# The first tile in halves, the small memory product in the start, and Wq and Wk one tile further ahead

## The chip, the cores and the metric

The kernel runs on one core of a Trainium2 chip. The time is device microseconds of one execution. Nearly all of it is work of TensorE. In the profile PE is TensorE (PEld its weight loads), DVE is VectorE, ACT is ScalarE, POOL is GpSimd, and SP is SyncE, which issues transfers. TensorE writes its results into banks of a memory called PSUM.

Two clocks are used. Lines of the profile count from the start of the span. Tables made from the trace count from the first warm-up matmul, which starts 1.38 us into the span in the kernel before. Such times are marked **W**.

## The reference, cut to what matters

```python
xn = _layernorm(x)                     # x: 2048 x 1024
out = x + A_ref(xn, mem0, Wq, Wk, Wv, Wo) + B_ref(xn, w1, w2, w3, w4)

# B_ref (mixer and MLP), the part that runs first:
h  = gelu(layernorm(xn) @ w1)          # "stage 1": 1024 x 1024 weights, 16 tiles of 128 tokens
hs = shifted(h) @ w2                   # "w2 stage"
x1 = xn + hs
b  = x1 + gelu(layernorm(x1) @ w3) @ w4

# A_ref: attention over segments of 32 tokens with 8 memory rows
h = concat([mem, xs]);  q, k, v = h @ Wq, h @ Wk, h @ Wv   # "V", then "attention" in five blocks
```

Of the kernel before, what the change touches and what calls it, by code (L numbers as in the profile page):

```python
# [23 lines left out]
P = 128  # L24
# [53 lines left out]
def kernel(  # L78
# [53 lines left out]
    ident = const_tile("c_ident", np.eye(P, dtype=np.float32))  # L132
    load_consts(1)
    eye9 = const_tile("c_eye9", np.concatenate([np.eye(M, dtype=np.float32), np.ones((M, 1), np.float32)], 1))
# [17 lines left out]
    nc.gpsimd.memset(sums[:], 1.0)  # L152
# [38 lines left out]
    with tc.manual_schedule(engines={mybir.EngineType.PE, mybir.EngineType.SP, mybir.EngineType.Pool}), ExitStack() as actx:  # L191
# [6 lines left out]
        with ExitStack() as bctx:  # L198
# [13 lines left out]
            with ExitStack() as hctx:  # L212
                psum0 = hctx.enter_context(tc.tile_pool(name="psum0", bufs=2, space=PSUM))
# [6 lines left out]
                with ExitStack() as p0:  # L220
# [7 lines left out]
                    def load_x(n):  # L228
                        if n < NT:
                            xts[n] = ring.tile([P, D], BF16, tag="xt", bufs=10, name=f"xt{n}")  # L230
                            nc.sync.dma_start(xts[n][:], x_v[:, n, :])

                    load_x(0)
# [13 lines left out]
                    def norm_stats(n, part=None):  # L247
# [14 lines left out]
                        nc.gpsimd.tensor_tensor(rr[:], ab[:], neghalf[:], op=ALU.pow)  # L262
# [26 lines left out]
                    def transposes(xn2, xn2T, jj, half, halves=False):  # L289
                        ps = psum0.tile([P, 4, P], F32, tag="tr")  # L290
                        for k in range(4):
                            nc.tensor.matmul(ps[:, k, :], xn2[:, (half * 4 + k) * P:(half * 4 + k + 1) * P], ident[:], start=True, stop=True)
                        step = 2 if halves else 4
                        for i in range(0, 4, step):
                            nc.scalar.copy(xn2T[:, jj, half * 4 + i:half * 4 + i + step, :], ps[:, i:i + step])
# [50 lines left out]
                    tr(0, 1, True)  # L346
                    norm_stats(1)
                    nc.gpsimd.memset(hTB[:, :, 0:2], 0.0)
                    nc.gpsimd.memset(hTB[:, :, S + 2:S + 4], 0.0)
                    load_consts(5)  # L350
# [12 lines left out]
                    def ahead(n):  # L363
# [3 lines left out]
                        norm1(n - 2)  # L367
# [5 lines left out]
                    def prep(n):  # L373
                        norm2_of(n)
                        norm_stats(n + 1)
                        norm1(n - 2)
# [38 lines left out]
            with ExitStack() as p3:  # L415
# [11 lines left out]
                def seg_sums(n):  # L427
# [3 lines left out]
                    with nc.allow_low_precision(reason="sums are accumulated in fp32 and rounded once"):  # L431
                        nc.vector.tensor_reduce(xb[:, :, 4 * n:4 * n + 4], xr[:].rearrange("p k (s t) -> p k s t", t=SEG), axis=AX.X, op=ALU.add)

                m0 = ring.tile([M, D], BF16, tag="nsq", bufs=1)
                nc.gpsimd.dma_start(m0[:], A_mem0[0])
                for c in range(7):
                    nc.sync.dma_start(w4_sb[:, 4 * c:4 * (c + 1), :], w4_v[:, 4 * c:4 * (c + 1), :])

                def mem_start():
                    ps9 = psum3.tile([P, KT, M + 1], F32, tag="vr")  # L440
                    for k in range(KT):
                        nc.tensor.matmul(ps9[:, k, :], m0[:, k * P:(k + 1) * P], eye9[:], start=True, stop=True)
                    nc.vector.tensor_copy(MZ[:, :, 0:M], ps9[:, :, 0:M])
                    nc.vector.tensor_tensor(xb[:, :, 0:1], ps9[:, :, M:M + 1], xb[:, :, 0:1], op=ALU.add)
# [83 lines left out]
                for tb in range(4):  # L528
# [18 lines left out]
                    for j in range(4):  # L547
# [16 lines left out]
                        elif n == 3:  # L564
                            mem_start()
# [168 lines left out]
        def stage_loads(Bs, hg, ready=()):  # L734

            cs_ = slice(hg * 512, (hg + 1) * 512)
            ws = [(w, None) for w in ready]
            ws += [(wtile(), src) for src in (Wq_v, Wk_v)[len(ready):]]
            (wq, _), (wk, _) = ws
            for w, src in ws[len(ready):]:  # L740
                for k0 in (0, 4):
                    loads.append(lambda w=w, src=src, k0=k0: nc.sync.dma_start(w[:, k0:k0 + 4, :], src[:, k0:k0 + 4, cs_]))
            return wq, wk
# [21 lines left out]
        ahead = stage_loads([nextB[0]], 0, first_w)  # L765
        for gi_, group in enumerate(groups):
# [3 lines left out]
            for hg in range(8):  # L770
# [3 lines left out]
                wq, wk = ahead  # L774
# [4 lines left out]
                if hg < 7:  # L779
# [239 lines left out]
```

## The kernel before: the parts that the change and the argument touch

Loads of the start. SP (`nc.sync`) and ScalarE (`nc.scalar`) issue them; w1 comes in quarters.

```python
def load_x(n):
    if n < NT:
        xts[n] = ring.tile([P, D], BF16, tag="xt", bufs=10, name=f"xt{n}")
        nc.sync.dma_start(xts[n][:], x_v[:, n, :])
load_x(0)
for c, q in ((0, nc.scalar), (2, nc.scalar), (1, nc.sync), (3, nc.sync)):
    if q is nc.sync:
        load_x(1 + c // 2)
    q.dma_start(w1_sb[:, 2 * c:2 * c + 2, :], w1_v[:, 2 * c:2 * c + 2, :])
# ... x tiles 3 to 6, w2 in quarters, x tiles 7 to 9; 10 to 12 follow in norm1
```

For each x tile: statistics on DVE, a power on POOL, and two normalisations. `norm2` is the input of stage 1. It runs on DVE up to tile 7 and on ScalarE from tile 8 on. Tiles 0 to 5 are then transposed by TensorE; from tile 6 on (`NPE = 6`) a **transposing transfer** (a DMA that transposes) issued by SP does it. `norm1` is kept for the residual, and stored to DRAM for attention.

```python
def norm2(n, xn2T, jj):
    xn2 = ring.tile([P, D], BF16, tag="xn2")          # three buffers
    if n < 8:
        ...                                           # DVE
    else:
        nc.scalar.activation(xn2[:], xts[n][:], ACTF.Identity, bias=nm2[:], scale=rr[:, 1:2])
    if n >= NPE:
        nc.sync.dma_start_transpose(xn2T[:, jj], xn2[:])

def norm1(n):
    xn = xn_keep[n // 4][:, n % 4]
    nc.vector.tensor_scalar(xn, xts[n][:], mv[:, 0:1], rr[:, 0:1], op0=ALU.subtract, op1=ALU.mult)
    nc.gpsimd.dma_start(xn_v[:, n, :], xn)            # 256 KB store

def transposes(xn2, xn2T, jj, half, halves=False):
    ps = psum0.tile([P, 4, P], F32, tag="tr")         # two banks
    for k in range(4):
        nc.tensor.matmul(ps[:, k, :], xn2[:, (half * 4 + k) * P:(half * 4 + k + 1) * P], ident[:], start=True, stop=True)
    step = 2 if halves else 4
    for i in range(0, 4, step):
        nc.scalar.copy(xn2T[:, jj, half * 4 + i:half * 4 + i + step, :], ps[:, i:i + step])

# stage 1 from tile 4 on takes two tiles at once; tile 9 is needed when tiles 8 and 9 start
stage1(3, 1, tiles2[2], {...: ahead(6) ... ahead(7)}, 1)
for n in range(13, NT):
    load_x(n)
def prep(n):
    norm2_of(n)
    norm_stats(n + 1)
    norm1(n - 2)
for n0 in range(4, NT, 2):
    ...                                               # prep(n0 + 4), prep(n0 + 5) between
    stage1(n0, 2, tiles2[n0], between)
```

The product of the memory rows with a small matrix (eight tiny matmuls, called `mem_start`) stands in the w4 stage. In attention the loads of Wq and Wk are made one group of heads ahead, into four buffers, and are put into SP's queue between the transposing transfers of the probabilities.

## Time and profile before

| | kernel before |
|---|---|
| times of its first three runs | 1509.06, 1513.19, 1509.02 us |
| span of the profiled run | 1507.1 us |
| TensorE busy | 1497.1 us |
| first stage 1 matmul (W) | 10.63 us |
| first w2 matmul (W) | 65.75 us |
| first V matmul (W) | 531.42 us |
| first matmul of attention's projections (W) | 752.44 us |
| first output matmul (W) | 873.86 us |

A landmark (when the first matmul of a stage starts) says how much time lies behind TensorE at that point. The difference of two landmarks is the length of a stage, holes included. The lines of the page, of the table of waits and of the order in time are shown and read in the prediction below. There `L305` is stage 1 of the first tile, `L315` stage 1, `L442` the eight small matmuls, `L658` the projections of attention.

### The profile page before, as it was taken

The numbers are of one execution on the slowest core, as the hardware profiler recorded it, in microseconds if no ns is written. First come the engines' busy times: TensorE is split into PE (matmuls) and PEld (weight loads), VectorE is DVE, ScalarE is ACT, GpSimd is POOL, SyncE is SP. The second block draws the span as 40 slices with busy tenths as digits, with TensorE's granted clock in tenths as the row PEclk, the third lists the DMA queues.
The fourth block names the chain that finished last, engine by engine and source line by source line (L and its number), as shares of the span: only waits on it lengthen the run. The fifth ranks groups of instructions, "written<-read, shape, count | busy, mean of one in ns | idle before, by whom it ended". The sixth has DMA issues, their size and how long they took to land.

```text
span 1507.1 us, 24242 instructions
## 1 busy us (share of the span) xinstructions
PE 1497.1 (99%) x9757; PEld 803.3 (53%) x9828; DVE 546.9 (36%) x1146; ACT 502.0 (33%) x1140; POOL 176.6 (12%) x247
## 2 busy tenths in 40 slices
PE   9999999999999999999999999999999999999999
PEld 7844444445454444444456645664665455545555
DVE  8382230100010112211246624651564166516642
ACT  5533103013012011111156614650663166406630
POOL 5241020211211221100000000001000100010001
PEclk9999999999999999999999999999999999999999
DMA  9699752453445777622389956992997298918911
GB/s 307 156 272 321 218 174 89 137 203 111 155 155 144 188 236 252 218 98 84 126 219 262 238 128 174 255 239 72 240 251 203 72 230 217 223 63 207 209 49 51
DMA packets 305410, 272.93 MB, mean 181 GB/s; under 512 B 156054, under 2 KB 272312, under 8 KB 305296
## 3 DMA queue, kind: packets, MB, share of 16 engines
q1 hardware_dynamic: 282800, 189.38, 50.4%
q0 software_dynamic: 21808, 80.85, 15.4%
q8 instruction: 79, 1.29, 0.4%
q10 hardware_dynamic: 688, 1.11, 0.2%
q14 instruction: 35, 0.29, 0.1%
HBM read 190.08 MB, written 45.29 MB: 156 GB/s over the span
## 4 chain that ended last, share of the span: by engine, by line
PE 98%; DVE 1%; issue 0%; DMA 0%; ACT 0%; POOL 0%
PE ps L658 30%; PE ps L592 15%; PE pso L716 15%; PE ps L533 13%; PE ps L559 13%; PE ps L397 4%; PE ps L315 3%; PE psS L673 2%; PE psO L697 2%; PE ps L856 1%; PE ps L485 1%; PE gps L468 0%; PE ps L454 0%; DVE st L256 0%; DVE st L259 0%
## 5 line engine op out<-in xcount | busy, mean ns | idle before, releaser
L658 PE MATMUL ps<-hTb,wt 128*128 128x396 bf16 (+2 forms) x2528 | 484.9, 342 | 0.0
L658 PEld LDWEIGHTS <-wt 128*128 128x128 bf16 x2528 | 236.7, 98 | 175.7 <-DMA wt<-in_A_Wq_dram 0.4
L592 PE MATMUL ps<-wt,xT 128*128 128x512 bf16 x1004 | 220.1, 379 | 1.1
L716 PE MATMUL pso<-wo_sb,oX 128*128 128x512 bf16 (+1 forms) x972 | 208.3, 372 | 1.1
L533 PE MATMUL ps<-xn3T,w_sb 128*128 128x512 bf16 x896 | 196.2, 379 | 0.0
L559 PE MATMUL ps<-w_sb,h3T 128*128 128x512 bf16 x873 | 194.1, 379 | 1.2
L592 PEld LDWEIGHTS <-xT 128*128 128x128 bf16 x1024 | 100.2, 98 | 120.8
L534 ACT ACTIVATE h3T<-ps 128x512 bf16<-128x512 f32 x112 | 66.9, 597 | 291.1 <-PE ps L533 290.2
L716 PEld LDWEIGHTS <-oX 128*128 128x128 bf16 x992 | 96.3, 98 | 107.6
L660 ACT CAST KT<-ps 128x462 bf16<-128x462 f32 (+2 forms) x160 | 81.8, 511 | 202.8 <-PE ps L658 198.7
L559 PEld LDWEIGHTS <-h3T 128*128 128x128 bf16 x896 | 87.1, 98 | 103.6
L533 PEld LDWEIGHTS <-w_sb 128*128 128x128 bf16 x896 | 86.6, 98 | 102.0
L679 DVE TENSOR_REDUCE sums<-sm 99x4 f32<-99x396 f32 (+2 forms) x176 | 97.6, 555 | 114.9 <-ACT sm L677 114.9
L662 ACT ACTIVATE QT<-ps 128x462 bf16<-128x462 f32 (+2 forms) x160 | 83.9, 525 | 120.3 <-PE ps L658 106.2
L594 ACT CAST Vs<-ps 128x512 bf16<-128x512 f32 x64 | 37.5, 586 | 232.1 <-PE ps L592 223.5
L675 DVE TENSOR_TENSOR sm<-psS,c_mask_reg_sb 99x396 f32<-99x396 f32 x152 | 86.7, 571 | 72.0 <-PE psS L673 71.7
L598 DVE CAST Vs<-ps 128x512 bf16<-128x512 f32 x64 | 44.3, 692 | 171.6 <-PE ps L592 166.0
L677 ACT ACTIVATE sm<-sm 99x396 f32<-99x396 f32 (+2 forms) x176 | 92.8, 527 | 34.9 <-DVE sm L675 27.9
L685 DVE TENSOR_TENSOR Pn<-sm,rs 99x396 bf16<-99x396 f32 (+2 forms) x176 | 98.9, 562 | 6.4 <-DVE rs L681 0.5
L723 POOL DMA_DIRECT2D out_dram<-ot x30 | 16.4, 548 | 698.2 <-DVE ot L722 698.1
L560 DVE TENSOR_TENSOR R<-ps,R 128x512 f32<-128x512 f32 x32 | 22.0, 690 | 182.1 <-PE ps L559 172.5
L722 DVE TENSOR_TENSOR ot<-pso,Rt 128x512 bf16<-128x512 f32 (+1 forms) x33 | 22.2, 675 | 166.6 <-PE pso L716 162.3
(127 smaller groups left out, 1049.5 us busy)
## 6 DMA issues: line engine op xcount, KB each, us to landing
wt<-in_A_Wq_dram SPq DMA_DIRECT2D x76, 512.0 KB
wt<-in_A_Wk_dram SPq DMA_DIRECT2D x76, 512.0 KB
wt<-in_A_Wv_dram POOLq DMA_DIRECT2D x24, 1024.0 KB, 6.4
V_scratch<-Vs SPq DMA_DIRECT2D x32, 512.0 KB
V<-V_scratch SPq DMA_DIRECT2D x40, 384.0 KB
R_scratch<-x POOLq DMA_DIRECT2D x16, 512.0 KB, 4.1
R<-R_scratch SPq DMA_DIRECT2D x16, 512.0 KB
R_scratch<-R POOLq DMA_DIRECT2D x16, 512.0 KB, 3.5
```

The lines of the kernel that those rows point to most:

```text
L533: nc.tensor.matmul(ps[:].rearrange("p (n t) -> p n t", t=P), w3_sb[:, k, f * P:(f + 1) * P], xn3T[tb][:, :, k, :], start=(k == 0), stop=(k ...
L534: nc.scalar.activation(h3T[:, f, :], ps[:], ACTF.Gelu_apprx_tanh)
L559: nc.tensor.matmul(ps[:], h3T[:, f, j * P:(j + 1) * P], w4_sb[:, f, ch * 512:(ch + 1) * 512], start=(f == 0), stop=(f == FT - 1))
L592: nc.tensor.matmul(ps[:], xT[:, m4 * 4 + j, k, :], wv[:, k, :], start=(k == 0), stop=(k == KT - 1))
L658: nc.tensor.matmul(ps[:, :nb], w[:, k, hh * P:(hh + 1) * P], B["hT"][:, k, :nb], start=(k == 0), stop=(k == KT - 1))
L660: nc.scalar.copy(dst[:, hh, :], ps[:, :nb])
L662: nc.scalar.mul(dst[:, hh, :], ps[:, :nb], scale)
L675: nc.vector.tensor_tensor(sm[:T, :, :T], S3, t["mask"][:].unsqueeze(1).to_broadcast((T, 4, T)), op=ALU.add)
L677: nc.scalar.activation(e[:T, :, :T], sm[:T, :, :T], ACTF.Exp, scale=LN2)
L679: nc.vector.tensor_reduce(ss, e[:T, :, :T], axis=AX.X, op=ALU.add)
L685: nc.vector.tensor_tensor(Pn[:T, :, :T], e[:T, :, :T], rs[:T, :].unsqueeze(2).to_broadcast((T, 4, T)), op=ALU.mult)
L716: nc.tensor.matmul(self.ps[:, :self.w], self.oX[0][:, h, self.oX[1] + self.gl * P:self.oX[1] + (self.gl + 1) * P], wo_sb[:, h, self.cc], s ...
```

## The change

Its intent: get the first tile through sooner (two half loads on two queues, an identity made on the core and not loaded, a power split in two, four PSUM banks for the transposes), move the eight small matmuls from the w4 stage into a hole at the start, take one `norm1` out of tile 9's path, and load Wq and Wk of attention one tile further ahead, with a fifth buffer in three blocks. The load of x tile 12 also moves to POOL's queue.

```diff
-    ident = const_tile("c_ident", np.eye(P, dtype=np.float32))
+    ident = cpool.tile([P, P], BF16)
+    nc.vector.memset(ident[:], 1.0)          # ... then affine_select on POOL
-                psum0 = hctx.enter_context(tc.tile_pool(name="psum0", bufs=2, space=PSUM))
+                psum0 = hctx.enter_context(tc.tile_pool(name="psum0", bufs=4, space=PSUM))
-                            nc.sync.dma_start(xts[n][:], x_v[:, n, :])
+                            if n == 0:
+                                nc.scalar.dma_start(xts[n][:, 512:], x_v[:, n, 512:])
+                                nc.sync.dma_start(xts[n][:, :512], x_v[:, n, :512])
+                            else:
+                                (nc.gpsimd if n == 12 else nc.sync).dma_start(xts[n][:], x_v[:, n, :])
-                        nc.gpsimd.tensor_tensor(rr[:], ab[:], neghalf[:], op=ALU.pow)
+                        for c in (slice(1, 2), slice(0, 1)) if n == 0 else (slice(0, 2),):
+                            nc.gpsimd.tensor_tensor(rr[:, c], ab[:, c], neghalf[:, c], op=ALU.pow)
 # transposes: one bank for each copy, not one for two
                     tr(0, 1, True)
+                    ps9 = psum.tile([P, KT, M + 1], F32, tag="mm", bufs=4, name="ps9")
+                    for k in range(KT):
+                        nc.tensor.matmul(ps9[:, k, :], m0[:, k * P:(k + 1) * P], eye9[:], start=True, stop=True)
 ...                                           # mem_start in the w4 stage is deleted
                     def prep(n):
                         norm2_of(n)
                         norm_stats(n + 1)
+                        if n == 8:
+                            norm1(n - 3)      # ahead(7) no longer does it
                         norm1(n - 2)
 ...
-                if hg < 7:
-                    ahead = stage_loads(Bs, hg + 1, ...)
+                while len(ws) < min(now + (5 if now < 44 else 4), 16 * len(SEGS)):
+                    load_w()                  # every fifth tile into the free buffer "oXb"
```

More of the change, by code (lines that the diff above doesn't have):

```diff
@@ L130, in load_consts @@
             nc.gpsimd.dma_start(t[:], d.ap())
-    ident = const_tile("c_ident", np.eye(P, dtype=np.float32))
-    load_consts(1)
-    eye9 = const_tile("c_eye9", np.concatenate([np.eye(M, dtype=np.float32), np.ones((M, 1), np.float32)], 1))
+    ident = cpool.tile([P, P], BF16)
+    nc.vector.memset(ident[:], 1.0)
+    eye9 = cpool.tile([M, M + 1], BF16)
+    c0 = cpool.tile([P, KT, 1], F32)
     mask_first = const_tile("c_mask_first", _tile_mask(3, True))
@@ L151 @@
     sums = cpool.tile([P, NTILE * 8, 4], F32)
-    nc.gpsimd.memset(sums[:], 1.0)
     SH = (-1, -1, 1, 1, -2, -2, 2, 2)
@@ L230, in load_x @@
                             xts[n] = ring.tile([P, D], BF16, tag="xt", bufs=10, name=f"xt{n}")
-                            nc.sync.dma_start(xts[n][:], x_v[:, n, :])
+                            if n == 0:
[3 more added lines that the diff above has]
+                                (nc.gpsimd if n == 12 else nc.sync).dma_start(xts[n][:], x_v[:, n, :])
+                    m0 = hTB[:M, 0, 16:16 + D]
+                    nc.gpsimd.dma_start(m0, A_mem0[0])
+                    nc.gpsimd.affine_select(ident[:], ident[:], [[-1, P]], ALU.is_equal, 0.0, base=0, channel_multiplier=1)
+                    nc.gpsimd.memset(eye9[:, M:M + 1], 1.0)
+                    nc.gpsimd.tensor_copy(eye9[:, 0:M], ident[:M, :M])
                     load_x(0)
@@ L289, in transposes @@
                     def transposes(xn2, xn2T, jj, half, halves=False):
-                        ps = psum0.tile([P, 4, P], F32, tag="tr")
-                        for k in range(4):
-                            nc.tensor.matmul(ps[:, k, :], xn2[:, (half * 4 + k) * P:(half * 4 + k + 1) * P], ident[:], start=True, stop=True)
                         step = 2 if halves else 4
                         for i in range(0, 4, step):
-                            nc.scalar.copy(xn2T[:, jj, half * 4 + i:half * 4 + i + step, :], ps[:, i:i + step])
+                            ps = psum0.tile([P, 4, P], F32, tag="tr")
+                            for k in range(step):
+                                c = (half * 4 + i + k) * P
+                                nc.tensor.matmul(ps[:, k, :], xn2[:, c:c + P], ident[:], start=True, stop=True)
+                            nc.scalar.copy(xn2T[:, jj, half * 4 + i:half * 4 + i + step, :], ps[:, :step])
                     def stage1_k(xn2T):
@@ L346 @@
                     tr(0, 1, True)
+                    ps9 = psum.tile([P, KT, M + 1], F32, tag="mm", bufs=4, name="ps9")
+                    for k in range(KT):
+                        nc.tensor.matmul(ps9[:, k, :], m0[:, k * P:(k + 1) * P], eye9[:], start=True, stop=True)
                     norm_stats(1)
+                    nc.vector.tensor_copy(MZ[:, :, 0:M], ps9[:, :, 0:M])
+                    nc.vector.tensor_copy(c0[:], ps9[:, :, M:M + 1])
                     nc.gpsimd.memset(hTB[:, :, 0:2], 0.0)
                     nc.gpsimd.memset(hTB[:, :, S + 2:S + 4], 0.0)
-                    load_consts(5)
+                    load_consts(4)
+                    nc.gpsimd.memset(sums[:], 1.0)
                     for n in range(1, 6):
@@ L366, in ahead @@
                         norm_stats(n + 1, 1)
-                        norm1(n - 2)
+                        if n == 6:
+                            norm1(n - 2)
                     stage1(3, 1, tiles2[2], {0: [lambda: tr(4, 0)], 2: [lambda: tr(4, 1), lambda: ahead(6)], 4: [lambda: tr(5, 0)], 5: [lambda: tr(5, 1), lambda: ahead(7)]}, 1)
@@ L432, in seg_sums @@
                         nc.vector.tensor_reduce(xb[:, :, 4 * n:4 * n + 4], xr[:].rearrange("p k (s t) -> p k s t", t=SEG), axis=AX.X, op=ALU.add)
-                m0 = ring.tile([M, D], BF16, tag="nsq", bufs=1)
-                nc.gpsimd.dma_start(m0[:], A_mem0[0])
+                    if n == 0:
+                        nc.vector.tensor_tensor(xb[:, :, 0:1], c0[:], xb[:, :, 0:1], op=ALU.add)
                 for c in range(7):
                     nc.sync.dma_start(w4_sb[:, 4 * c:4 * (c + 1), :], w4_v[:, 4 * c:4 * (c + 1), :])
-                def mem_start():
-                    ps9 = psum3.tile([P, KT, M + 1], F32, tag="vr")
-                    for k in range(KT):
-                        nc.tensor.matmul(ps9[:, k, :], m0[:, k * P:(k + 1) * P], eye9[:], start=True, stop=True)
-                    nc.vector.tensor_copy(MZ[:, :, 0:M], ps9[:, :, 0:M])
-                    nc.vector.tensor_tensor(xb[:, :, 0:1], ps9[:, :, M:M + 1], xb[:, :, 0:1], op=ALU.add)
                 def unit_vb(hg):
@@ L563 @@
                                 spec_step(depth)
-                        elif n == 3:
-                            mem_start()
                         elif n > 3:
@@ L732, in load_some, with load_w @@
                 loads.pop(0)()
-        def stage_loads(Bs, hg, ready=()):
+        ws = first_w + second_w
+        def load_w():
+            n = len(ws)
+            src, hg = (Wq_v, Wk_v)[n % 2], n // 2 % 8
             cs_ = slice(hg * 512, (hg + 1) * 512)
-            ws = [(w, None) for w in ready]
-            ws += [(wtile(), src) for src in (Wq_v, Wk_v)[len(ready):]]
-            (wq, _), (wk, _) = ws
-            for w, src in ws[len(ready):]:
-                for k0 in (0, 4):
-                    loads.append(lambda w=w, src=src, k0=k0: nc.sync.dma_start(w[:, k0:k0 + 4, :], src[:, k0:k0 + 4, cs_]))
-            return wq, wk
+            ws.append(abig.tile([P, KT, 512], BF16, tag="oXb", name=f"w{n}") if n < 48 and n % 5 == 3 else wtile())
+            for k0 in (0, 4):
+                loads.append(lambda w=ws[-1], k0=k0: nc.sync.dma_start(w[:, k0:k0 + 4, :], src[:, k0:k0 + 4, cs_]))
         def tick(us, blocked=None):
@@ L764 @@
         nextB = {b: block_setup(b) for b in groups[0]}
-        ahead = stage_loads([nextB[0]], 0, first_w)
         for gi_, group in enumerate(groups):
@@ L773 @@
                     load_some(len(loads))
-                wq, wk = ahead
+                now = 16 * gi_ + 2 * hg
+                wq, wk = ws[now:now + 2]
                 QTs = [qkv.tile([P, 4, B["nb"]], BF16, tag="QT", name=f"QT{B['b']}") for B in Bs]
@@ L778 @@
                     nextB = {b: block_setup(b) for b in groups[gi_ + 1]}
-                if hg < 7:
-                    ahead = stage_loads(Bs, hg + 1, second_w if (gi_, hg) == (0, 0) else ())
-                if hg == 7 and gi_ + 1 < len(groups):
-                    ahead = stage_loads([nextB[b] for b in groups[gi_ + 1]], 0)
+                while len(ws) < min(now + (5 if now < 44 else 4), 16 * len(SEGS)):
+                    load_w()
                 Vs = [qkv.tile([P, len(B["tiles"]), 512], BF16, tag="V", bufs=3, name=f"V{B['b']}") for B in Bs]
```

## The prediction

> **What bounds the kernel now.** I read the page's busy shares first, then the table of who TensorE waited for, then the order in time of the places where it waited.
>
> ```profile
> PE 1497.1 (99%) x9757; PEld 803.3 (53%) x9828; DVE 546.9 (36%) x1146; ACT 502.0 (33%) x1140; POOL 176.6 (12%) x247
> PE warm L332 <- DVE wz L326: 1.4, 1, 1.4
> PE ps L292 <- DVE xn L271: 0.8, 1, 0.8
> PE ps L315 <- ACT hTB L317: 0.5, 1, 0.5
> PEld L442 <- issue: 0.4, 1, 0.4
> PEld L658 <- DMA wt<-in_A_Wq_dram: 0.4, 1, 0.4
> ```
>
> TensorE is busy for 1497.1 of 1507.1 us, and a busy TensorE need not be at its rate, so I checked the rate: I took the start-to-start distance of all consecutive matmuls in the trace and subtracted columns/2.4 GHz + 2.5 ns. Counting the places where a matmul record is plainly missing as no loss, what is left over in the whole run is: 0.96 us between the last warm-up matmul and the first transpose (5.96 to 7.14), 0.30 us between the transposes and the first real matmul (7.64 to 7.99), 0.6 us at 31.4 to 32.2, 0.34 us around the eight small matmuls of L442 at 219 us, and a spread of under 0.25 us per pair of lines elsewhere. After the last matmul there is the output's tail to 1507.1, which the change does not touch. So all that any change of order can win here is about 2.2 us, 0.15% of the time. The wait for Wq in the second wait table is on the weight load; no pair of matmul starts around 789 us, where it falls, is further apart than its columns explain (one pair has 167 ns, exactly one missing record). Weight loads run ahead, so that wait was hidden.
>
> The start, in order of time for TensorE:
>
> ```profile
> 1.38 4.96 PE L332 MATMUL warm<-wz 128*128 128x512 bf16 x12 [1.38 <-DVE wz L326]
> 7.14 0.72 PE L292 MATMUL ps<-c_ident_sb,xn 128*128 128x128 bf16 x8 [0.79 <-DVE xn L271]
> 7.99 2.84 PE L305 MATMUL ps<-xn2T,w_sb 128*128 128x128 bf16 x48
> 10.67 0.61 PE L292 MATMUL ps<-c_ident_sb,xn 128*128 128x128 bf16 x8
> 11.12 1.06 PE L305 MATMUL ps<-xn2T,w_sb 128*128 128x128 bf16 x16
> ...
> 4.03 0.69 DVE L256 BATCH_NORM_STATS2 st<-xt 128x6 f32<-128x512 bf16 x1 [2.71 <-DMA xt<-in_A_x_dram]
> ```
>
> The reader is to see that the path to the first transpose is x tile, statistics, power on POOL, normalisation; and that from 7.99 us on TensorE runs without a hole. The DMA side of the same stretch (last columns: granted clock, DMA share, GB/s):
>
> ```profile
> 2.00:3.00 1.00, 1.00 (x3) 0.30 (x2) 0.00 (x0) 1.00 (x1) 0.61 (x1) 1.00 0.78 178
> 3.00:4.00 1.00, 1.00 (x4) 0.39 (x3) 0.00 (x0) 0.25 (x2) 0.00 (x0) 1.00 0.99 377
> 8.00:10.00 2.00, 2.00 (x36) 2.00 (x36) 1.11 (x5) 0.77 (x3) 0.83 (x4) 1.00 1.05 389
> ```
>
> From 3 us on the DMA engines are full, at 377 to 389 GB/s. The trace's semaphore increments give the landings: x tile 0 at 4.01, the four quarters of w1 at 5.28, 8.79, 8.54 and 10.83 us (in the order in which TensorE needs them). It needs them at 7.99, 7.99+16x0.056=8.88, 9.78 and 11.12. The second and the last have 0.1 and 0.3 us to spare.
>
> **What the Trainium skill says.** "TensorE: Matmul & The Clock Gate", section "Wait — 56ns, not 53.3ns?", gives N/2.4 GHz plus about 2.5 ns start to start when warm. The trace agrees: fifty 512-column matmuls from 67.57 to 78.36 us are 215.8 ns each; my bound of 2.2 us rests on it. "DMA: Bandwidth & Descriptors", section "Issuing engines are not separate DMA queues", says transfers issued by scalar, sync and gpsimd run on the same 16 DMA engines and interleave, so a second issuer saves only issue time. The trace agrees: with two issuers active the sum stays at 377 to 389 GB/s. "Perfetto Trace Analysis", section "Matmuls", wants independent groups in different PSUM banks so that evacuation overlaps the next group. Here the first ScalarE copy starts at 7.57, after all four transposes of its bank, which is what two copies out of one bank look like. "GPSIMD Engine Reference", section "2.1 Instruction dispatch", puts about 6 us on the first call after a library is loaded. The trace bounds that lower: the pool configuration is at 2.53 us and the first power starts at 5.91, 0.08 us after its input, so at most 3.3 us.
>
> **The change part by part.**
>
> First tile. x tile 0 comes as two halves of 128 KB on two queues, ahead of w1. Today the first 128 KB of it have been started by 2.57 us and the second only by 3.49. I expect the first statistics at about 3.3 and the second at about 3.9 (today 4.63), an estimate from those packet times. The power on POOL is split; one of one column takes 0.57 us (L405) against 0.73 for two, 0.16 less. So the first transpose moves from 7.14 by 0.7+0.16 to about 6.3, just where the warm-up matmuls leave TensorE (last one started at 5.96). The eight L442 matmuls (8x0.035=0.28 us) are put after the transposes, where TensorE has its 0.30 us hole anyway, so the first real matmul still comes about 0.85 us after the first transpose: about 7.2 instead of 7.99. But the last quarter of w1 must be there for the last sixteen of those matmuls. All bytes ahead of it are the same 2.8 MB through the same full engines, so it lands near 10.8 again, and the L305 matmuls that start at 11.12 today can start at about 10.9. **Gain 0.2 to 0.25 us, not 0.8.** The identity is now made on POOL, not loaded, and has until about 6 us; the transfer of the identity landed at 6.6 us, so this had to go for the transposes to start earlier.
>
> L442 moved. At 219 us it cost 0.34 us. In its new place it is hidden. **Gain 0.34 us.** One DVE addition and two small copies from PSUM fall into DVE's 0.8 us waits for the power.
>
> The stall at 31.4 us. TensorE waits for a bank that ScalarE frees:
>
> ```profile
> 30.64 1.24 ACT L273 ACTIVATE xn<-xt,nm,rr 128x1024 bf16<-128x1024 bf16 x1 [2.05 <-DVE mv L260]
> 31.79 0.91 ACT L317 ACTIVATE hTB<-ps 128x256 bf16<-128x256 f32 x3
> 32.20 35.09 PE L315 MATMUL ps<-xn2T,w_sb 128*128 128x256 bf16 x320 [0.54 <-ACT hTB L317]
> ```
>
> ScalarE sat 2.05 us before the normalisation of tile 8 (L273), in order, with the eviction behind it. The releaser named is DVE, but the wait just before it in ScalarE's queue ended at 30.56, and 30.54 is when the transposing transfer of tile 6 landed, 5.57 us after its issue at 24.96. It was issued as soon as tile 6 was normalised. DVE's chain runs about 0.6 us earlier in the new kernel, TensorE only 0.2, so the transfer lands at about 29.95 and the eviction ends near 31.6 where TensorE asks at 31.46. Moving the normalisation of tile 5 behind tile 9's statistics takes 0.54 us of DVE off tile 9's path, not off tile 8's, so it adds nothing to this wait. **Gain about 0.4 of the 0.54 us.**
>
> Wq and Wk one tile ahead. Loads per stage are the same, each buffer is freed at the same place; the fifth buffer exists only because a tile lies idle in blocks 0 to 2. It removes the 0.4 us wait of the weight load, which cost TensorE nothing. **Gain 0 to 0.1 us.**
>
> Sum: 0.2+0.34+0.4+0.1=1.04, so 1509.06-1.1=**1508.0 us**.
>
> **The rivals.** (1) The transfers don't bind at the start: two queues fill the engines before 3 us, where they moved only 178 GB/s, and the last quarter of w1 lands 0.5 us earlier. Then the start gives up to 0.8 us and the stall is fully gone: 1507.1. Against it: the scalar queue's first packet came only at 2.95 us although issued at 0.76. (2) The start gives nothing: the library load stands ahead of the identity's making on POOL, and the power waits for it; or the quarter of w1 at 8.79 (0.1 us to spare) stalls TensorE, and the transpose transfer still takes its 5.6 us: only L442's 0.34 us remains, 1508.7. (3) The longer look-ahead of Wq and Wk matters in runs that the profile did not show: one of the three runs took 1513.19, and if that was a late weight tile, the new kernel loses this tail but not the median. (4) SBUF or queue order makes a new wait in attention; the lists of instructions show SP's loads only moved earlier, so I give it little.
>
> **Range and chances.** TensorE's floor puts the best case near 1506.8; nothing in the change adds TensorE work, so the worst is about the time of before plus the spread of runs, 0.3 us. Eight in ten: 1507.0 to 1509.2. A change of 2% would need 30 us, fifteen times the whole loss: same 0.985, and one run in a hundred for something unforeseen that slows.
>
> **What would show it.** First transpose near 6.3 and first L305 matmul near 7.2; a new short hole before the L305 matmuls of the last quarter of w1, released by its transfer; no small matmuls at 219 us; the wait for ScalarE at 31 us below 0.2 us; no Wq wait near 789 us and otherwise the same attention. The prediction is wrong if that hole is absent (rival 1), if the first transpose stays after 7 us (rival 2), or if attention changes by more than 0.2 us.

## The result, and the profile after

Six runs of each kernel, with the kernel before at 1509.69 us median (1509.02 to 1513.19) and the changed one at **1509.2 us median** (1508.82 to 1510.15). The ratio is 0.9994, with a 95% interval of 0.9981 to 1.0007. A ratio is the mean time of one kernel's fast runs over that of the other's of the same rounds, so it is not quite the ratio of the medians. With the later calls there are 11 runs of the changed kernel (mean 1509.48, median 1509.39) and 38 of the kernel before (mean 1509.84): 0.35 us less, with a standard error of 0.23 us from the spread of the runs. That is below the 1.1 us forecast, and not clearly different from nothing. About 0.15 us of it lies outside the profiled span: the time is 2.04 to 2.20 us longer than the span before, and 1.91 to 1.99 us after.

The page of the changed kernel shows the same TensorE work:

```profile
PE 1497.4 (99%) x9757; PEld 803.7 (53%) x9828; DVE 547.0 (36%) x1148; ACT 502.1 (33%) x1140; POOL 175.5 (12%) x250
```

Its table of waits, TensorE's rows (total us, times, longest), answers to the one of before:

```profile
PE warm L343 <- DVE wz L337: 1.5, 1, 1.5
PE ps L316 <- DMA w_sb<-in_B_w_dram: 1.0, 1, 1.0
PE ps L326 <- DMA xn2T<-xn: 0.9, 1, 0.9
PE psO L708 <- ACT KT L671: 0.5, 1, 0.5
```

Of the waits shown of before only the warm-up's is left, and three others have come: for a quarter of w1, for a transposing transfer, and one in attention. The profiled run took 1510.15 us and was the slowest of the six, so a second profile was needed before believing any of them. First the start of this one, in order of time, TensorE only:

```profile
6.57 0.79 PE L305 MATMUL ps<-ident,xn 128*128 128x128 bf16 x8
7.29 0.35 PE L360 MATMUL ps<-eye,hTB 8*128 8x9 bf16 x8
7.58 1.07 PE L316 MATMUL ps<-xn2T,w_sb 128*128 128x128 bf16 x16
9.64 1.96 PE L316 MATMUL ps<-xn2T,w_sb 128*128 128x128 bf16 x32 [0.99 <-DMA w_sb<-in_B_w_dram]
11.44 0.61 PE L305 MATMUL ps<-ident,xn 128*128 128x128 bf16 x8
11.88 1.06 PE L316 MATMUL ps<-xn2T,w_sb 128*128 128x128 bf16 x16
```

The transposes start at 6.57 (7.14 before), the eight small matmuls fit behind them, and the first real matmul comes at 7.58 (7.99 before). Then TensorE waits for the second quarter of w1. Its sixteen semaphore increments came spread from 7.22 to 9.59 us; in the kernel before they came from 8.28 to 8.79. The windows of the same stretch (last columns: granted clock, DMA share, GB/s):

```profile
2.00:3.00 1.00, 1.00 (x4) 0.33 (x3) 0.00 (x0) 0.72 (x1) 0.53 (x4) 1.00 0.74 245
3.00:4.00 1.00, 1.00 (x3) 0.30 (x2) 0.43 (x1) 0.76 (x2) 0.00 (x0) 1.00 1.04 273
8.00:10.00 2.00, 1.01 (x19) 0.83 (x17) 1.18 (x5) 0.23 (x1) 1.44 (x5) 1.00 1.05 405
```

The transfers move 245 GB/s at 2 to 3 us where they moved 178. At 8 to 10 us the transfers are full, as before, and TensorE is idle for half of it. The second new wait with a cause in view is in attention's first block (order in time, DVE and TensorE):

```profile
797.81 0.57 DVE L696 TENSOR_TENSOR Pn<-sm,rs 99x396 bf16<-99x396 f32 x1 [1.19 <-DMA PT<-Pn]
797.85 0.34 PE L708 MATMUL psO<-PT,V 99*128 99x99 bf16 x4 [0.55 <-ACT KT L671]
```

DVE waited 1.19 us for a transposing transfer of probabilities to free its buffer, and TensorE lost 0.71 us (start-to-start distance less the columns' time) just then.

### The profile page after: what moved, and what is told of

It is laid out like the page before. It is cut to its first block, busy times and chain, and to the rows that moved or that the text cites. A ratio compares the mean times of both kernels' runs of the same rounds, so it can differ in the third digit from the quotient of the medians.

```text
span 1508.2 us, 24250 instructions
## 1 busy us (share of the span) xinstructions
PE 1497.4 (99%) x9757; PEld 803.7 (53%) x9828; DVE 547.0 (36%) x1148; ACT 502.1 (33%) x1140; POOL 175.5 (12%) x250
## 4 chain that ended last, share of the span: by engine, by line
PE 98%; DMA 1%; issue 0%; SPq 0%; ACT 0%; DVE 0%
PE ps L669 30%; PE ps L603 15%; PE pso L727 15%; PE ps L546 13%; PE ps L572 13%; PE ps L417 4%; PE ps L326 3%; PE psO L708 2%; PE psS L684 2%; PE ps L865 1%; PE ps L498 1%; DMA w_sb<-in_B_w_dram 1%; PE ps L467 0%; PE gps L481 0%; DMA xn2T<-xn 0%
## 5 line engine op out<-in xcount | busy, mean ns | idle before, releaser
L669 PE MATMUL ps<-hTb,wt 128*128 128x462 bf16 (+2 forms) x2272 | 439.6, 344 | 0.0
L669 PEld LDWEIGHTS <-wt 128*128 128x128 bf16 x2272 | 212.7, 98 | 159.9
```

Source lines behind the costliest of these rows:

```text
L669: nc.tensor.matmul(ps[:, :nb], w[:, k, hh * P:(hh + 1) * P], B["hT"][:, k, :nb], start=(k == 0), stop=(k == KT - 1))
```

## The experiments

All kernels gave correct results. Each is run for five rounds (four in two cases), beside the kernel before. Two readings carry the argument: the landmarks, and **holes**, which are start-to-start distances of TensorE's matmuls less columns/2.4 GHz + 2.5 ns, with plainly missing records left out.

### 1. The changed kernel and the kernel before once more

No edit. This is for a second profile of each.

> The changed kernel itself again, for a second profile and five more times. Theory A (the hole at 8.4 us behind the second quarter of w1, and the 1.1 us stall at 39 us behind a transposing transfer, are luck of one execution, the slowest of three): here both are smaller, together under 1.0 us, the first w2 matmul comes less than 66.3 us after the first warm-up matmul (it was 66.83), and the median is under 1509.0. Theory B (both belong to the new order of transfers): both are there again at 0.7 us or more each, the first w2 matmul at 66.5 to 67, the median 1509 to 1509.5.

> The kernel before itself, for a second profile and the noise of one comparison. First w2 matmul 65.6 to 66.0 us after the first warm-up matmul (65.75 in its first profile) if its start is repeatable; over 66.3 if the start wanders from execution to execution by as much as the change moved it. Ratio to itself within 0.0007 of 1.

Changed kernel again: 1509.88 us median, above the ranges of both theories, ratio 1.0 (0.9987 to 1.0014). Kernel before again: 1509.98, ratio to itself 1.0006 (0.9992 to 1.002), and its first w2 matmul at W 66.03, 0.03 above the expected range. TensorE at the start of the changed kernel, second profile:

```profile
6.59 0.72 PE L305 MATMUL ps<-ident,xn 128*128 128x128 bf16 x8 [0.15 <-DVE xn L281]
7.24 0.35 PE L360 MATMUL ps<-eye,hTB 8*128 8x9 bf16 x8
7.53 2.89 PE L316 MATMUL ps<-xn2T,w_sb 128*128 128x128 bf16 x48
10.25 0.61 PE L305 MATMUL ps<-ident,xn 128*128 128x128 bf16 x8
10.83 1.07 PE L316 MATMUL ps<-xn2T,w_sb 128*128 128x128 bf16 x16
```

The wait for the second quarter is gone (it landed at W 6.93, for 8.12 in the first profile): so late a landing was of one execution. What stays is the short hole before 10.83, where the last sixteen matmuls wait for the last quarter of w1. It landed at W 9.30, and they start at W 9.35.

The stall in stage 1 did not go. Kernel before, second profile, ScalarE and TensorE:

```profile
30.92 1.24 ACT L273 ACTIVATE xn<-xt,nm,rr 128x1024 bf16<-128x1024 bf16 x1 [2.57 <-DMA xn2T<-xn]
32.48 9.77 PE L315 MATMUL ps<-xn2T,w_sb 128*128 128x256 bf16 x88 [1.06 <-ACT hTB L317]
```

Changed kernel, second profile, the same two engines:

```profile
29.95 1.24 ACT L283 ACTIVATE xn<-xt,nm,rr 128x1024 bf16<-128x1024 bf16 x1 [1.63 <-DVE ab L270]
39.90 2.34 PE L326 MATMUL ps<-xn2T,w_sb 128*128 128x256 bf16 x20 [1.24 <-DMA xn2T<-xn]
```

In before ScalarE's normalisation of tile 8 waits for tile 6's transposing transfer, ScalarE's eviction stands behind it, and TensorE loses 1.22 us at W 30. In the changed kernel ScalarE starts 1 us sooner and TensorE loses only 0.29 us there. But 7 us later it loses 1.41 us, now directly for a transposing transfer, that of tile 9. Theory A (luck) falls for stage 1 and holds for the start; the first w2 matmul, at W 66.36 for 66.83, lies between what the two expected.

### 2. Each half of the change alone

Look-ahead only: the last part of the diff on the kernel before. Start only: the rest of the diff.

```diff
 # look-ahead only: before, with
+                while len(ws) < min(now + (5 if now < 44 else 4), 16 * len(SEGS)):
+                    load_w()
 # start only: the changed kernel, with
-                while len(ws) < min(...): load_w()
+                if hg < 7:
+                    ahead = stage_loads(Bs, hg + 1, ...)
```

> The kernel before with only the Wq and Wk look-ahead of the change. If the look-ahead is worth nothing, as predicted (0 to 0.1 us): 1509.1 to 1509.7 and its profile has no stall of TensorE over 0.3 us in attention. If its earlier loads make the new 0.7 us stall at 797 us (a transposing transfer of attention slowed by weights): the same stall here and 0.5 us more time, with the w2 landmark as in before (65.75).

> The change without the Wq and Wk look-ahead. If the start as such is what costs and L442's removal what gains: first w2 matmul near 66.8 as in the changed kernel, V first near 532.1, no stall at 797 us, so about 0.5 us faster than the changed kernel if the look-ahead made that stall: 1508.6. If the look-ahead is worth nothing: the same 1509.2 as the changed kernel.

Look-ahead only: 1510.36 us, ratio 1.0007 (0.9993 to 1.002). Start only: 1509.36 us, ratio 0.9998 (0.9984 to 1.0012). These totals are within each other's noise and settle neither expectation; the landmarks say more. Look-ahead only has before's start (first stage 1 matmul at W 10.36) and no stall at 797 us; start only has the changed start (10.12) and a hole of just 0.15 us at 795. So neither half alone makes the attention stall in these two profiles.

### 3. What gates stage 1: theory G against its rivals

At this point the six profiles gave a pattern. From the landing of tile 9's transposing transfer (its sixteenth semaphore increment) to the first w2 matmul it is 28.08 us in four of them. In the two where TensorE came to tile 9 later than the transfer, it is a little more. The matmul starts 0.13 to 0.15 us after the landing wherever there is a hole of over 0.2 us at W 37 or 38. That gave **theory G**: the landing of tile 9, near W 38.1, sets when the w2 stage starts, and it is pinned by the volume of transfers that run at the same time. The rivals: tile 8's buffer is the whole cause (H), or a transposing transfer takes 6 us whatever else moves.

First edit, on the kernel before: the three xn2 buffers strictly in turn. The allocator had given tile 8 the buffer of tile 6, which the transposing transfer reads.

```diff
-                        xn2 = ring.tile([P, D], BF16, tag="xn2")
+                        xn2 = ring.tile([P, D], BF16, tag=f"xn2{n % 3}", bufs=1, name=f"xn2_{n}")
```

> The kernel before, but the buffers of xn2 are given out strictly in turn, so that tile 8's normalisation on ScalarE writes over tile 5 (read by TensorE) and no longer over tile 6, whose reader is the transposing transfer that lands at 29.4 us after the first warm-up matmul. Both theories: the stall at 29.8 (1.22 us in the second profile of before) falls to 0.3 or less. Theory G (the landing of tile 9's transposing transfer gates stage 1, and it is pinned near 38.1 us by the volume of transfers): the wait comes back at 37 us, 0.7 us or more, the first w2 matmul is again 28.1 us after that landing, at 65.9 to 66.3, no gain. Rival H (the buffer of tile 8 is the cause of all of stage 1's loss): no wait of over 0.3 us at 37, first w2 matmul at 65.0 to 65.3, 0.8 us faster than before.

1509.55 us, ratio 1.0002 (0.9989 to 1.0016). The hole at W 30 fell from 1.22 to 0.13 us, and the time came back as a hole of 1.01 us at W 37:

```profile
39.52 6.71 PE L315 MATMUL ps<-xn2T,w_sb 128*128 128x256 bf16 x60 [0.85 <-ACT hTB L317]
```

The releaser named is ScalarE, but tile 9 landed at W 38.01 and this matmul starts at W 38.14, the 0.13 us of the other profiles. The first w2 matmul came at W 66.09, again 28.08 after the landing. A wait was removed and nothing gained, as G had it; H falls.

Second edit: the loads of x tiles 13 to 15 behind tile 9's transposing transfer, not ahead of tile 8's, on both kernels. Third: both edits on the changed kernel.

```diff
-                    for n in range(13, NT):
-                        load_x(n)
                     def prep(n):
 ...
                         norm1(n - 2)
+                        if n == 9:
+                            for m in range(13, NT):
+                                load_x(m)
```

> The changed kernel with the loads of x tiles 13 to 15 (768 KB) issued after tile 9's transposing transfer and not ahead of tile 8's. Theory G (tile 9's landing near 38.1 is set by the transfers it shares the engines with): it lands 1 to 2 us earlier, at 36.2 to 37.2, the wait at 37 us falls from 1.4 to under 0.4, the first w2 matmul comes at 65.0 to 65.5, 0.8 to 1.2 us less than 66.36. Rival (each transposing transfer takes 6 us behind the other one whatever else moves): tile 9 lands at 38 again and the first w2 matmul stays at 66.2 to 66.5.

> The kernel before with the same move of x tiles 13 to 15. Theory G: in before ScalarE's late eviction at 29.8 us holds TensorE 1.2 us, so it does not come to tile 9 before 38.0 anyway; the stall at 29.8 stays near 1.2, the one at 37 (0 to 0.23) goes, first w2 matmul 65.8 to 66.0 against 66.03, no measurable gain. If instead it gains 0.7 us or more, the two stalls share one cause and theory G is too simple.

> The changed kernel with both: buffers of xn2 in turn, x tiles 13 to 15 late. Theory G: no wait over 0.3 us in stage 1, first w2 matmul at 64.7 to 65.1 us, which is 0.8 us before the best profile of the kernel before; time 1508.4 median or below (changed kernel 1509.2 to 1509.9), with whatever the stall at 795 us in attention costs still in it (0.7 in both profiles of the changed kernel).

On the changed kernel tile 9 landed at W 37.40, the hole at 37 shrank to 0.47 us, and the first w2 matmul came at 65.46. With both edits it landed at 36.25, the hole went, and w2 began at **65.05**. Both w2 landmarks are within what was expected of G (the first one's landing is 0.2 us later than its range, its hole 0.07 us longer). The totals did not follow: 1509.18 us, ratio 0.9998 (0.9985 to 1.0012), and 1509.64 us, ratio 1.0007 (0.9993 to 1.0021), the second with one run of 1514.32. This is the nearest to a version that beats both kernels, and the totals do not show that it does.

On the kernel before the expectation failed in the profile: the first w2 matmul came at W 69.30, not 65.8 to 66.0. The five runs had a median of 1509.9 us, ratio 1.0 (0.9986 to 1.0013), and the profiled one, at 1513.37 us, is the outlier; the other four (1508.55 to 1510.12 us) have no profile, so what the edit does in a usual execution stays unknown. The hole at W 30 went as well, because tile 6 landed at 28.54 (29.44 in the second profile of before), and a much larger one came for tile 11, whose transfer, now behind the three loads, took 10.1 us from issue to landing (W 36.41 to 46.53). The profile shows what such an outlier can be made of. TensorE first, then the windows:

```profile
48.05 8.16 PE L315 MATMUL ps<-xn2T,w_sb 128*128 128x256 bf16 x58 [2.33 <-DMA xn2T<-xn]
```

```profile
46.00:48.00 2.00, 0.00 (x0) 0.00 (x0) 1.93 (x6) 0.39 (x2) 1.35 (x3) 1.00 1.27 120
48.00:50.00 2.00, 1.95 (x16) 1.66 (x17) 0.72 (x2) 0.39 (x1) 1.90 (x4) 0.85 1.14 361
50.00:54.00 4.00, 4.00 (x26) 3.08 (x25) 0.00 (x0) 2.28 (x4) 1.08 (x3) 0.65 0.90 296
54.00:58.00 4.00, 4.00 (x39) 3.60 (x37) 0.00 (x0) 2.74 (x6) 0.00 (x0) 1.00 1.03 282
```

TensorE stood still for 2.50 us, ran 1.5 us at full rate, and then fifteen matmuls of 256 columns started 213 ns apart and not 109: a granted clock of 0.85 and 0.65 in those windows. That is 1.6 us more. So this stall cost over half as much again in clock. The stalls of 1.1 to 1.4 us had no such tail.

### 4. The stores taken out of stage 1

The strongest test of G: the sixteen 256 KB stores of `norm1` leave stage 1, and are issued by POOL beside the first four tiles of the w2 stage, just after a stretch in which the transfers were idle.

```diff
-                        nc.gpsimd.dma_start(xn_v[:, n, :], xn)
 # in the loop of the w2 stage:
+                        if n < 4:
+                            for m in range(4 * n, 4 * n + 4):
+                                nc.gpsimd.dma_start(xn_v[:, m, :], xn_keep[n][:, m % 4])
```

It ran on the changed kernel, on the one with the start only, and on the kernel before. A fourth run also gives the Wq and Wk loads of block 0 to POOL:

```diff
-                loads.append(lambda w=ws[-1], k0=k0: nc.sync.dma_start(...))
+                loads.append(lambda w=ws[-1], k0=k0, q=nc.gpsimd if n < 16 else nc.sync: q.dma_start(...))
```

> The changed kernel with the sixteen 256 KB stores of the normalised x tiles taken out of stage 1 and issued beside the first four tiles of the w2 stage, where the transfers are idle (share 0.01 at 66 to 72 us). Five of these stores (25.0 to 34.8 us) share the engines with the transposing transfers of tiles 6 to 9. Theory G (the volume of transfers pins tile 9's landing at 38.1 us): it lands at 35 to 37, the wait at 37 us is under 0.2, the first w2 matmul at 64.7 to 65.1 us after the first warm-up matmul (66.36 and 66.83 without the edit), time 1508.2 median or below. Rival (DVE or ScalarE pins it): landing still 37.5 to 38.7, first w2 matmul 66 or later.

> The same edit without the Wq and Wk look-ahead. Stage 1 as in the kernel with the look-ahead, first w2 matmul 64.7 to 65.1. In attention, if the look-ahead's loads on the SP queue make the stall at 794 to 797 us (0.36 to 0.71 in four profiles with look-ahead and the new start): no wait over 0.2 us there, and 0.3 to 0.6 us less between the first projection matmul and the first output matmul (121.4 against 121.9). If the stall is luck: as often here.

> The kernel before with the same edit. If the gate is gone in both, what the change saves at the start passes through: the first w2 matmul comes 0.15 to 0.35 us later here than in the changed kernel with the edit, at 64.9 to 65.4, and from there to the first V matmul 465.66 us here against 465.28 there, so 0.5 to 0.7 us between the two kernels in all, where the kernels without the edit showed none. If the start gain is lost elsewhere: the same w2 landmark in both.

> The changed kernel with deferred stores, and the Wq and Wk loads of block 0 issued by POOL, not SP. If the stall at 794 to 797 us comes from SP issuing those loads ahead of the transposing transfers of P in its queue: gone (under 0.15 us), first projection to first output matmul 121.2 to 121.4 us. If it comes from the bytes of these loads on the engines: still 0.3 us or more. Rival: POOL's issues delay its other work in block 0 and a new wait comes; then over 122.

As kernels all four are failures: 1523.04 us (ratio 1.0096), 1524.73 (1.0087), 1529.01 (1.0126) and 1525.97 (1.0115). The stores met the 512 KB stores of the w2 stage. In the first of them, DVE and TensorE:

```profile
104.92 0.69 DVE L417 TENSOR_TENSOR x<-ps,xnk 128x512 f32<-128x512 f32 x1 [5.06 <-DMA R_scratch<-x]
```

```profile
105.67 2.72 PE L416 MATMUL ps<-w_sb,hTB 128*128 128x512 bf16 x6 [4.68 <-DVE x L417]
```

DVE waited 5.06 us for a store to free its buffer, TensorE 4.68 for DVE, and the clock fell again (granted clock 0.50 from 105.6 to 108 us). Yet stage 1, which comes before all that, is a clean measurement. Two windows of the changed kernel:

```profile
34.00:36.00 2.00, 2.00 (x21) 1.79 (x20) 1.93 (x6) 1.78 (x4) 1.79 (x3) 1.00 1.26 143
38.00:40.00 2.00, 1.42 (x14) 1.03 (x11) 1.93 (x6) 1.98 (x4) 1.70 (x3) 1.00 1.20 329
```

The same windows without the stores:

```profile
34.00:36.00 2.00, 2.00 (x21) 1.80 (x19) 1.97 (x5) 1.53 (x4) 1.19 (x2) 1.00 0.69 132
38.00:40.00 2.00, 2.00 (x21) 1.79 (x19) 1.93 (x6) 0.80 (x3) 1.15 (x2) 1.00 0.68 130
```

The DMA share falls from 1.26 and 1.20 to 0.69 and 0.68 (a share over 1 means that packets overlapped on an engine), and TensorE has no hole. DVE is as busy as ever, 1.93 to 1.97 of 2 us, so DVE was not the gate. The transposing transfers of tiles 9 and 10 took 7.09 and 6.92 us from issue to landing with the stores, and 3.10 and 3.05 without. POOL, which no longer issues the stores and is less busy, wasn't the gate either: tile 9's transfer was issued at W 31.49, only 0.17 us sooner, and landed 4.2 us sooner. Whether the bytes of the stores count, or their packets' time on the engines, was not separated. All profiles of the kernels, on clock W:

| kernel | last quarter of w1 landed | its first matmul | first stage 1 matmul | hole at 30 | hole at 37-38 | tile 9 landed | first w2 matmul | landing to w2 |
|---|---|---|---|---|---|---|---|---|
| before | 9.45 | 9.74 | 10.63 | 0.70 | under 0.13 | 37.48 | 65.75 | 28.27 |
| before, again | 9.24 | 9.49 | 10.39 | 1.22 | under 0.13 | 37.84 | 66.03 | 28.19 |
| look-ahead only | 9.20 | 9.47 | 10.36 | 1.23 | 0.23 | 38.17 | 66.25 | 28.08 |
| before, buffers in turn | 9.37 | 9.63 | 10.52 | 0.13 | 1.01 | 38.01 | 66.09 | 28.08 |
| before, no stores | 9.22 | 9.60 | 10.49 | none | none | 35.24 | 64.92 | 29.68 |
| changed | 10.15 | 10.41 | 11.30 | under 0.13 | 1.10 | 38.75 | 66.83 | 28.08 |
| changed, again | 9.30 | 9.35 | 10.25 | 0.29 | 1.41 | 38.28 | 66.36 | 28.08 |
| start only | 9.17 | 9.22 | 10.12 | 0.55 | 1.06 | 38.08 | 66.16 | 28.08 |
| changed, x late | 9.40 | 9.51 | 10.40 | 0.11 | 0.47 | 37.40 | 65.46 | 28.06 |
| changed, both edits | 9.36 | 9.41 | 10.31 | none | none | 36.25 | 65.05 | 28.80 |
| changed, no stores | 9.37 | 9.47 | 10.37 | none | none | 34.59 | 64.79 | 30.20 |
| start only, no stores | 9.39 | 9.44 | 10.35 | none | none | 34.52 | 64.77 | 30.25 |

(The outlier of section 3 and the fourth run here, 10.33 and 64.76, are left out.) Three things are read from it. Where the transfers gate, 28.08 us is the length of stage 1 behind tile 9's landing. Where they do not, in the kernels without stores, stage 1 is 54.42 or 54.43 us long (64.79 less 10.37, 64.92 less 10.49). With both edits it is 54.74: TensorE lost another 0.26 us at W 44.1, 0.13 us after the transfer of tile 11 landed. And only without the stores does the gain of the start come through: the w2 stage begins 0.13 to 0.15 us earlier with the changed start than with the old one (0.03 to 0.05 from the start of the span). The expectation for the pair without stores, 0.15 to 0.35 us, was slightly high; its second half, 465.66 us to the first V matmul, could not be read, as the w2 stage was disturbed in all four kernels.

From the first w2 to the first V matmul, which holds the w4 stage, it is 465.66 or 465.67 us in five profiles with the eight small matmuls there, and 465.27 or 465.28 in five without: **0.39 us**, the most repeatable number.

Attention's first block, from the first projection matmul to the first output matmul, takes 121.24, 121.56, 121.60, 121.86, 121.95 and 121.96 us with the look-ahead (mean 121.70), and 121.24, 121.25, 121.39, 121.41, 121.42, 121.47 and 121.91 without (mean 121.44). The ranges overlap; the look-ahead looks 0.25 us worse, and that is not settled. The pair without stores differs by 0.09 us only (121.56 with, 121.47 without; expected 0.3 to 0.6). Giving its loads to POOL made it 123.92, by a wait for a weight tile of its own:

```profile
784.89 1.36 PE L671 MATMUL ps<-hTb,wk 128*128 128x403 bf16 x7 [2.18 <-DMA wk<-in_A_Wk_dram]
```

So the hole at 797 us could not be pinned on SP's queue by that test: the rival it named, a new wait, came instead.

## Why the prediction was right or wrong

**What bounds the kernel: right.** TensorE's work sets the time, and only some 2 us of holes could be won. The list of holes came from one execution, though. The kernel before, profiled again, had 0.55 us where the list says 0.96, and 1.22 where it says 0.6. (The first trace itself has 0.70 there: 810 ns between two matmuls, where 109 is the rule.) The list also leaves out a hole of 0.17 us, told under Wq and Wk below.

**First tile: mechanism right, size too high.** The last quarter of w1 lands near 9.3 in either kernel (9.20 to 9.51 with the old start, 9.17 to 9.40 with the new one, the late run aside). The new start has TensorE waiting for it, 0.05 to 0.11 us after the landing, where the old one came 0.25 to 0.38 after it. The gain is this slack: between the medians of six and eight profiles (10.51 and 10.34) it is 0.17 us on clock W, predicted 0.2 to 0.25. But the prediction's times count from the start of the span, and there the later warm-up takes 0.10 us back: 0.07 us is left (medians 11.89 and 11.82), a third of the forecast. The transposes came at 6.35 to 6.59 in the eight profiles, not 6.3, and the first real matmul at 7.28 to 7.85, not 7.2; the wait for w1 hides that. Rival 2 had pointed at the quarter with 0.1 us to spare. It did stall TensorE, by 1.16 us in one profile of the eight, and by 0.52, 0.23 and 0.12 in three others. The identity and the power on POOL did not hold anything up, and rival 1 (the transfers don't bind) was wrong.

**The eight small matmuls: right.** 0.34 us predicted, 0.39 measured. The 0.34 is the hole alone; the columns' time of the eight matmuls, eight times 6.25 ns, is the other 0.05.

**The stall in stage 1: this step failed.** The text said that the transfer of tile 6 would land sooner and that this would give "about 0.4 of the 0.54 us". It did land sooner: issued at 24.41 us for 24.96, landed at 29.69 for 30.54, and the hole there shrank from 0.70-1.23 to 0.00-0.55 us. But the time was not won. Tile 9 was issued 0.7 to 1.1 us sooner too (W 31.7 to 31.8 for 32.5 to 32.75), which the text had also foreseen, and its transfer then took 6.3 to 7.1 us for 5.0 to 5.4, since it still shared the engines with the loads of x tiles 13 to 15 and the stores. One store had even moved towards it: that of tile 5 went with its `norm1`, from W 28.6-28.9 to 30.0. That this move is not needed for the effect is seen in the kernel before with buffers in turn, where it had not moved (W 28.68): tile 9, issued at 31.93, took 6.08 us and landed at 38.01. In the changed kernel it landed at 38.1 to 38.8, no sooner than before. TensorE, now earlier, waited there for 1.06 to 1.41 us. The step counted a wait removed as time won, without asking which wait stands next on the same path. That next gate was fixed by the transfers on the same engines, so it took back all of the 0.4 us and the start's gain as well: stage 1 got longer by about 0.4 us (from 55.12, 55.64, 55.89 to 55.53, 56.11, 56.04). Runs without the stores show it directly.

**Wq and Wk: this step failed too.** The weight load's wait is gone, but it had not been worth nothing. The prediction put 167 ns between two matmuls down to a missing record. The kernel before, TensorE and its weight loads:

```profile
787.25 1.53 PE L658 MATMUL ps<-hTb,wt 128*128 128x403 bf16 x8
788.79 1.71 PE L658 MATMUL ps<-hTb,wt 128*128 128x403 bf16 x8
789.64 0.46 PEld L658 LDWEIGHTS <-wt 128*128 128x128 bf16 x4 [0.40 <-DMA wt<-in_A_Wq_dram]
```

The second group has all its eight matmuls, as the first has, and takes longer; the matmul behind the late weights starts with them, at 789.64. The first block is longer by the same 0.17 us: 121.42 and 121.41 us in the two profiles of before, and 121.24 and 121.25 in two variants of it where the hole is absent. So the wait cost TensorE 0.17 us, above the 0 to 0.1 that was forecast. The cost side is larger: in both profiles of the changed kernel the block takes 121.95 and 121.96 us, 0.54 more than before, by the hole of 0.71 us at 797, less the 0.17 saved. That is over the 0.2 us at which the prediction called itself wrong, and it was given "little" under rival 4. Over all profiles the loss looks like 0.25 us, and its cause stays open. Rival 3, that the look-ahead removes outliers, is neither shown nor refuted: 3 of 38 runs of before were over 1511 us and none of 11 of the changed kernel, but a variant with the look-ahead had one of 1514.32. The one outlier caught in a profile was a late transposing transfer, not a late weight tile.

**The sum.** From the landmarks: start 0.07 (from the start of the span) and small matmuls 0.39 won, stage 1 about 0.4 and attention perhaps 0.25 lost, so nothing won, against 0.35 less (standard error 0.23) by the clock. The two do not contradict each other, as the profiles are of single runs: those of the changed kernel took 1510.15 and 1509.88 us, which is slow for it (median 1509.39), and those of before 1509.15 and 1509.24, which is fast for it (median 1509.69). The predicted 1508.0 us was 1.2 below the measured median of 1509.2, which is the upper edge of the range. That it lies inside is luck: the median of all 11 runs, 1509.39, lies outside. (The parts add up to 1.04, and 1.1 was taken off.) That it is the same time within 2% was never in doubt.

**How the skill served.** "DMA: Bandwidth & Descriptors", section "Issuing engines are not separate DMA queues", was read for the start, where it held: two queues, full engines, the last quarter no sooner. The same sentence, that transfers from all issuers interleave on the same 16 engines, decides stage 1, where stores from POOL stretch SP's transposing transfer of tile 9 from 3.1 to between 6.6 and 7.1 us. There it was not applied.

## What to carry to other kernels

Before a removed wait is booked as a gain, look for the next thing that the same engine will wait for and ask what fixes its time; if that is a transfer that others on the same engines hold up, arriving earlier only lengthens the wait. Before a gap is called a missing record, count the matmuls of its group. Landmarks in several profiles of both kernels resolve a tenth of a microsecond where totals resolve one. And move transfers only into a stretch that has room for all of them: the stretch beside the w2 stage's stores did not, and cost 13 to 19 us.

## What the Trainium skill lacked or had wrong

- "TensorE: Matmul & The Clock Gate", section "HAM oscillation — how this bites in real kernels", gives the rule "no PE-idle gaps >~3.4µs". Here a gap of 2.50 us was followed by a slow stretch: 1.5 us after it, fifteen 256-column matmuls ran 213 ns apart and not 109. In the kernel before without the stores, gaps of 2.74 and 2.46 us were followed, after 0.4 and 0.5 us, by 512-column matmuls 427 ns apart and not 216. A gap of 2.34 us (the run with Wq and Wk on POOL) and those of 1.1 to 1.4 us were not.
- "DMA: Bandwidth & Descriptors", section "DMA Transpose (X-bar)", lists constraints but no time. The skill has bandwidths and the time of a 128 x 128 one elsewhere, but nothing from issue to landing at the size used here, and nothing beside other transfers. Here one of 128 x 1024 bf16 (256 KB), on-chip to on-chip, took 3.0 to 3.1 us from issue to landing when little else ran, and 6.3 to 7.1 us (tile 9) beside 256 KB loads and stores.
- No page read here gives how far apart the 16 semaphore increments of one transfer may come: a quarter of w1 (512 KB) had its first at W 5.75 and its last at W 8.12 us in one execution, at 6.53 and 6.93 in another of the same kernel, and TensorE waited 1.16 us for the first.
- "GPSIMD Engine Reference", section "2.1 Instruction dispatch", has some 6 us for the first call after a library load. In the kernel before, the power is the first POOL instruction behind the pool configuration (2.53 us) and starts at 5.91, so it was at most 3.4 us, and its input came only at 5.83. In the changed kernel another POOL instruction starts at 2.10, 0.1 us behind the configuration at 2.00, so no such cost is seen. Which library was loaded, the trace does not say.
